# The first tokens of a transformer block: shorter Newton steps, two tiles normalised on their own, another order of the first products, and two more low parts on GpSimd

## The chip, the cores and the metric

The kernel runs on one core of one Trainium2 chip. The metric is device time in microseconds (us); the time before is 2038.93 us, the median of three runs (2038.71, 2038.93 and 2042.29).

The engines have short names below, as in the profile: PE is TensorE (matrix products and transposes), PEld its weight loads, DVE is VectorE, ACT is ScalarE, POOL is GpSimd, and SP issues most of the DMAs. Each engine works through its own queue of instructions in order and waits on semaphores for the others.

## The reference

One transformer block in float32 with 2048 tokens of 640 features, 32 heads of 20 and a feed-forward width of 1728:

```python
def _layernorm(x, axis=-1, eps=1e-5):
    m = jnp.mean(x, axis=axis, keepdims=True)
    v = jnp.var(x, axis=axis, keepdims=True)
    return (x - m) / jnp.sqrt(v + eps)

h = x + attention(_layernorm(x), wqkv) @ wo         # softmax(q k^T / sqrt(20)) v, 32 heads
h2 = h + (silu(z @ w_gate) * (z @ w_up)) @ w_down   # z = _layernorm(h)
```

## The kernel before

The tokens are cut into 16 tiles of 128 (one SBUF tile `xs[t]` of 128 x 640 each) and these into four chunks `c` of four tiles (`TPC`). Features are cut into five groups of 128 (`ND`).

Products of full float32 precision are made from two roundings: each operand `a` is kept as `a_hi`, a copy in the format fp32r, and `a_lo = a - a_hi`; a product is `a_hi w_hi + a_lo w_hi + a_hi w_lo`. The helper `split` (line 87) makes both: ACT copies to `hi`, then DVE (or POOL, by an argument) subtracts to `lo`; its instructions carry lines 88 and 89. A low part on DVE or POOL can only start behind ACT's high part.

The layer norm of a chunk takes, for each tile, `stats` (line 121): two BATCH_NORM_STATS2 over the halves of the 640 features and one BATCH_NORM_AGGREGATE into `mv`. Then `rstd_steps` (line 91) builds a list of functions that compute `r = 1/sqrt(var + eps)` for all tiles of the chunk together: `v = var + eps`, a first guess from the bits of `v`, and three Newton steps of four operations, so 14 in all; all these carry line 98. Then each tile is normalised in place (line 475), transposed on PE (`flip_tokens`, line 525; products at 529) and split into the high and low part of its columns of `z`.

**The opening** is at lines 715 to 739. SP issues the loads of four tiles of x and eight loads of `wqkv`; POOL sets the constant rows of `k_stk` (`fill_ones`, line 140, two memsets of 32 partitions x 4096). PE runs three warm-up products (line 721), which read the last tile of the chunk. `norm(0)` runs its whole list on DVE: statistics of four tiles, 14 Newton operations, four normalisations. The first two columns of weights (blocks m = 0 and 1) get their `w_hi` from ACT (line 727). Then each tile is transposed and split in turn; ahead of the last tile stands `first_blocks((0, 0))`, and after it the low parts of the weights of blocks 0 and 1 on DVE (line 734).

`first_blocks` (line 611) computes the first key block and the first query block, in two halves of 256 tokens. A pair `(h, n)` is half `h` (tokens of tiles 0 and 1, or 2 and 3) with operand pair `n`: 0 is `z_hi w_hi`, 1 is `z_lo w_hi`, 2 is `z_hi w_lo`; each pair is ten products (line 621). The remaining five pairs are issued at the first slot of the main loop (line 781). After them PE goes on with the other blocks (`query_key` and `rounds`, line 568), a stream without a pause by design.

`split_w` (called in the main loop) splits the weights of the further blocks m = 2, 3, ...: high part on ACT, low part on DVE for m < `LATE` and on POOL from `LATE` (6) on. `load_w` brings the weights in pairs of blocks into four slots, so a load on SP's queue waits until the low parts of the pair that had the slot are done. `keep` stores a finished block: a high and a low part, the latter for the widened key on POOL, and DMAs on POOL's queue to `k_d` and `q_d`.

A planner (`clock`, `takes`, `visit`) decides at build time where PE's stream takes the work of the attention's first maxima, and where a later chunk's normalisation steps go.

**Later users of the same function.** `projection` (line 886 on) uses `rstd_steps` for the second layer norm of chunks 0 to 2, during or right behind the attention, in three groups of at most five operations. `late_tokens` (line 1675 on) uses it for chunks 2 and 3 together, 8 tiles, during the first feed-forward elements: `moments` returns the list, one `apply` is added, and the loop `step` works off seven entries of this list `soon` at a time, then one entry of a list `late` at a time; these entries normalise (line 1705), transpose (line 1722) and store the late tokens.

Of the kernel before, what the change touches and what calls it, by code (L numbers as in the profile page):

```python
# [9 lines left out]
F32 = mybir.dt.float32  # L10
# [7 lines left out]
P = 128  # L18
# [5 lines left out]
ND = D // P  # L24
# [20 lines left out]
def tile_block(ctx: ExitStack, tc: tile.TileContext, x, wqkv, wo, wg, wu, wd, out):  # L45
# [41 lines left out]
    def split(src, hi, lo, lo_engine=nc.vector):  # L87
        nc.scalar.activation(hi, src, AF.Copy)  # L88
        lo_engine.tensor_tensor(out=lo, in0=src, in1=hi.bitcast(F32), op=ALU.subtract)  # L89

    def rstd_steps(pool, var, n, tag, engine=nc.vector):

        v = pool.tile([P, n], F32, name="v_" + tag)
        r = pool.tile([P, n], F32, name="r_" + tag)
        t = pool.tile([P, n], F32, name="t_" + tag)

        def some(f, *args, **kw):
            return lambda: f(*args, **kw)

        ts, tt = engine.tensor_scalar, engine.tensor_tensor  # L100
        guess = [
            some(nc.vector.tensor_scalar, v, var, EPS, None, op0=ALU.add),
            some(
                nc.vector.tensor_scalar, r.bitcast(I32), v.bitcast(I32), -0.5, 1597463007.0, op0=ALU.mult, op1=ALU.add
            ),
        ]
        better = [
            some(tt, out=t, in0=r, in1=r, op=ALU.mult),
            some(tt, out=t, in0=t, in1=v, op=ALU.mult),
            some(ts, t, t, -0.5, 1.5, op0=ALU.mult, op1=ALU.add),  # L110
            some(tt, out=r, in0=r, in1=t, op=ALU.mult),
        ]
        return r, guess + better * 3
# [4 lines left out]
            f()  # L118
        return r

    def stats(pool, src, mv):
        st = pool.tile([P, 2, 6], F32, name="st")
        for i in range(2):
            nc.vector.bn_stats(st[:, i, :], src[:, i * HALF : (i + 1) * HALF])
        nc.vector.bn_aggr(mv, st)


    NU = NG * NC
# [181 lines left out]
    with tc.tile_pool(name="pa", bufs=2) as pa:  # L310
# [99 lines left out]
        seconds, steps_due = [], [0]  # L410
        LANDING, LANDING_FIRST, SLACK, GATE, APART = 8000, 14000, 0, 500, 2500
        flips = []
        LATE, CHAIN = 6, 3000
        X_LANDING, x_there = 15000, [0]
        next_load = [0]

# [51 lines left out]
        def norm(c):  # L468

            mv = pa.tile([P, TPC, 2], F32, name="mv")  # L470
            engine, name = (nc.gpsimd, "POOL") if c else (nc.vector, "DVE")
            r, steps = rstd_steps(pa, mv[:, :, 1], TPC, "a", engine)

            def apply(t):
                nc.vector.tensor_scalar(
                    xs[c * TPC + t], xs[c * TPC + t], mv[:, t, 0:1], r[:, t : t + 1],
                    op0=ALU.subtract, op1=ALU.mult,
                )

            return (  # L480
                [
                    ("DVE", 1000, lambda t=t: stats(pa, xs[c * TPC + t], mv[:, t, :]))
                    for t in range(TPC)
                ]
                + [
                    (name if n else "DVE", 700 if n and c else 400, lambda f=f, g=g: (f(), g()))
                    for n, (f, g) in enumerate(zip(steps[::2], steps[1::2]))
                ]
                + [("DVE", 620, lambda t=t: apply(t)) for t in range(TPC)]
            )  # L490

        def flip(c, n):
# [19 lines left out]
            for b in range(2):  # L512
# [9 lines left out]
                nc.gpsimd.tensor_tensor(out=lo, in0=copy, in1=hi.bitcast(F32), op=ALU.subtract)  # L522
                takes("POOL", 4.8 * columns, clock["ACT"])

        def flip_tokens(t):

            ps = ps_wide().rearrange("p a b -> p (a b)")[:, :D]
            for k in range(ND):
                nc.tensor.transpose(
                    ps[:, k * P : (k + 1) * P], xs[t][:, k * P : (k + 1) * P], ident  # L530
                )
            ps = ps.rearrange("p (k n) -> p k n", k=ND)
            split(ps, *(z[:, :, t * P : (t + 1) * P] for z in zs[0]))

        stores = []

# [181 lines left out]
            load_w(i)  # L718
        warm = ps_one()
        for _ in range(3):  # L720
            nc.tensor.matmul(warm, ident, xs[TPC - 1][:, :CH], start=True, stop=True)
        for _, _, f in norm(0):
            f()
        zs[0] = z_tiles(0)
        first_raw = raws.pop(0), raws.pop(1)
        for m, raw in enumerate(first_raw):
            nc.scalar.activation(w_hi[:, :, m * P : (m + 1) * P], raw, AF.Copy)
        for t in range(TPC):
            flip_tokens(t)
            if t == TPC - 2:  # L730
                first_blocks((0, 0))
        for m, raw in enumerate(first_raw):
            cs = slice(m * P, (m + 1) * P)
            nc.vector.tensor_tensor(
                out=w_lo[:, :, cs], in0=raw, in1=w_hi[:, :, cs].bitcast(F32), op=ALU.subtract
            )
        load_w(4)
        loaded = 5
        split_at = (0, 4, 6, 7, 8, 9, 10, 11, 12, 13)
# [6 lines left out]
        for c in range(NC):  # L746
# [7 lines left out]
            for j, (kind, *which) in enumerate(work):  # L754
                slot[0] = 18 * c + j
                while flips and not j:
                    flips.pop(0)()
                if c == 0 and j < 9:
                    for i in range(split_at[j], split_at[j + 1]):
                        split_w(i + 2)  # L760
                        if i % 2 == 1 and loaded < 8:
                            load_w(loaded)
                            loaded += 1
                if c + 1 < NC and j == 0:
                    es[:0] = [
                        t.rearrange("p k n -> p (k n)")[:, : 2 * EW].rearrange(
                            "p (i n) -> p i n", i=2
                        )
                        for t in z_tiles(c + 1)
                    ]  # L770
                    if c:
                        es[:] = es[2:] + es[:2]
                if c + 1 < NC and j == 10:
                    es[:] = [e for e in es if any(e is own for own in own_es)]
                if j == (0 if c else 3) and c + 1 < NC:
                    load_x(c + 1)
                    x_there[0] = clock["PE"] + X_LANDING
                    lns = norm(c + 1)
                if which:
                    if (c, j) == (0, 0):  # L780
                        first_blocks((0, 1), (1, 0), (1, 1), (0, 2), (1, 2))
                        for m, ps in enumerate(firsts):
                            keep(0, m, ps)
                    else:
                        (query_key if kind == "block" else value)(c, *which)
                else:
                    flip_ctx.close()
                    psum = ps_ctx.enter_context(
                        tc.tile_pool(name="psum", bufs=1, space=bass.MemoryType.PSUM)
                    )  # L790
                    turn, jobs = [0], [0]

                    def ps_one():
                        jobs[0] += 1
                        return psum.tile([P, CH], F32, name="ps_one", tag=f"ps_{jobs[0] % 3}")

                    def ps_max():
                        n = turn[0] % 5
                        turn[0] += 1
                        if n > 2:  # L800
                            return psum_two.tile([P, CH], F32, name="ps_max", tag="ps_two")
                        return psum.tile([P, CH], F32, name="ps_max", tag="ps_max", bufs=3)

                if c == 0 and j == 6:
                    for ev in evs:
                        nc.gpsimd.memset(ev, 1.0)
                if (c, j) in ((1, 14), (1, 16), (2, 4), (3, 4)):
                    n = c if c > 1 else (j - 14) // 2
                    load_keys(0, slice(n * CH, (n + 1) * CH))
                if (c, j) in ((1, 15), (2, 0), (2, 9)):  # L810
                    load_queries(len(queries))
                if 0 in ends:
                    finish_at = min(finish_at, slot[0] + 2)
                    if slot[0] == finish_at:
                        max_finish(0)
                if j == 15 and c == 3:
                    load_values(0)
                if clock["PE"] >= x_there[0]:
# [1076 lines left out]
```

## Time and profile before

| | |
|---|---|
| median of three runs | 2038.93 us |
| profiled execution, its time | 2038.82 us |
| profiled execution, its span | 2037.0 us |
| DMA, mean over the span | 152 GB/s |
| PE, instructions | 14322 |
| POOL, instructions | 1103 |

The span runs from the first to the last instruction. A row of the timeline gives the start in us from the span's start, the length in us, the engine, the line, the operation, the tile written and the tiles read, the shape and the number of instructions merged into the row; in brackets stands the engine's idle time before it and what ended that. A row that merges several instructions gives the length of all together. A group in the list of costliest groups ends with its busy time and the mean of one instruction in ns. The list of waits says for an engine and line what it waited for: us in total, times, the longest in us.

### The profile page before, as it was taken

How to read it: one execution, taken by the hardware profiler on the slowest of the kernel's cores; microseconds unless marked ns; L12 is line 12 of the kernel's file. 1: busy time of each engine (PE TensorE's matmuls, PEld its weight loads, DVE VectorE, ACT ScalarE, POOL GpSimd, SP SyncE). 2: the span in 40 equal slices, each digit the busy share in tenths (PEclk: the TensorE clock that was granted, in tenths of full speed). 3: DMA queues.
4: the chain of work that ended last, by engine and by line, in shares of the span. 5: the costliest groups of instructions: out<-in, count | busy, mean ns of one | idle time of the engine just before them, and what ended most of it. 6: DMA issues, size and time to landing. Idle time of an engine off the chain costs nothing.

```text
span 2037.0 us, 40049 instructions
## 1 busy us (share of the span) xinstructions
PE 2012.7 (99%) x14322; PEld 1249.9 (61%) x14322; DVE 1607.9 (79%) x2826; ACT 1445.2 (71%) x2855; POOL 774.1 (38%) x1103
## 2 busy tenths in 40 slices
PE   8999999999999999999999999999999999999999
PEld 6989995343334333334333433345598888888888
DVE  5677778888888888888888888886378666676677
ACT  4677778999999999999999999987633222211221
POOL 6464423334342444352400011011146454754555
PEclk9999999999999999999999999999999999999999
DMA  7877563452634534435512131311158654974542
GB/s 244 255 244 260 175 206 89 116 161 79 187 104 124 166 115 143 149 127 176 156 46 79 27 94 44 92 62 55 33 184 302 220 192 157 344 273 158 202 150 94
DMA packets 194062, 310.01 MB, mean 152 GB/s; under 512 B 47760, under 2 KB 82576, under 8 KB 192840
## 3 DMA queue, kind: packets, MB, share of 16 engines
q1 hardware_dynamic: 187272, 283.85, 43.0%
q0 software_dynamic: 6496, 23.60, 4.0%
q8 instruction: 114, 1.87, 0.4%
q14 instruction: 84, 0.69, 0.1%
q10 hardware_dynamic: 96, 0.00, 0.0%
HBM read 207.75 MB, written 98.83 MB: 151 GB/s over the span
## 4 chain that ended last, share of the span: by engine, by line
PE 87%; DMA 3%; DVE 1%; issue 1%; POOL 1%; ACT 1%; SPq 1%; ACTq 0%; DVEq 0%; POOLq 0%
PE acc L1197 24%; PE ps_one L1187 16%; PE ps_a L1358 15%; PE ps_max L244 12%; PE ps_b L1452 8%; PE ps_one L568 6%; PE ps_max L211 2%; PE ps_max L918 2%; PE ps_b L918 1%; DMA units<-w_d 1%; DMA halves<-j_d 0%; DMA h<-in_A_x 0%; PE ps_max L953 0%; DVE tmp L1573 0%; ACT o L1207 0%
## 5 line engine op out<-in xcount | busy, mean ns | idle before, releaser
L1193 ACT ACTIVATE probs<-ps_one 128x512 f32<-128x512 f32 x2048 | 1056.7, 614 | 62.3 <-PE ps_one L1187 37.6
L250 DVE TENSOR_REDUCE mx<-ps_max 128x1 f32<-128x512 f32 x1472 | 926.2, 684 | 106.9 <-PE ps_one L1187 75.6
L1187 PE MATMUL ps_one<-q_stk,k_stk 62*128 62x512 f32 x2048 | 586.0, 450 | 2.8 <-DVE m L89 1.8
L1197 PE MATMUL acc<-probs,v_stk 128*32 128x512 f32 x4096 | 545.2, 604 | 0.0
L1187 PEld LDWEIGHTS ps_one<-q_stk,k_stk 62*128 62x128 f32 x2048 | 251.5, 184 | 432.7 <-ACT probs L1193 398.3
L244 PE MATMUL ps_max<-k_stk,q_stk 60*128 60x512 f32 x1472 | 381.2, 425 | 0.0
L244 PEld LDWEIGHTS ps_max<-k_stk,q_stk 60*128 60x128 f32 x1472 | 271.6, 186 | 24.1 <-DVE mx L250 0.9
L1573 DVE TENSOR_TENSOR tmp<-ps_a,tmp 128x512 f32<-128x512 f32 x208 | 141.2, 689 | 120.3 <-PE ps_a L1358 94.6
L233 DVE TENSOR_REDUCE mx<-ps_max 128x2 f32<-128x512 f32 x288 | 180.6, 685 | 66.5 <-PE ps_max L211 63.4
L1232 POOL TENSOR_TENSOR o<-o,rb 128x512 f32<-128x512 f32 x31 | 39.9, 1287 | 413.3 <-DMA q_stk<-q_d 241.5
L1197 PEld LDWEIGHTS acc<-probs,v_stk 128*32 128x32 f32 x4096 | 80.6, 108 | 174.8 <-issue 166.2
L223 ACT ACTIVATE ps_max<-ps_max 128x512 f32<-128x512 f32 x288 | 151.7, 583 | 47.5 <-PE ps_max L211 44.7
L1452 PE MATMUL ps_b<-halves,yp 128*128 128x320 f32 x1032 | 179.3, 308 | 2.0 <-DMA halves<-j_d 1.2
L1452 PEld LDWEIGHTS ps_b<-halves,yp 128*128 128x128 f32 x1032 | 165.1, 188 | 18.6 <-POOL yp L89 1.5
L1358 PE MATMUL ps_a<-t,units 128*128 128x512 f32 x624 | 162.6, 396 | 0.0
L1358 PE MATMUL ps_a<-z,units 128*128 128x512 f32 x516 | 133.9, 394 | 0.0
L89 POOL TENSOR_TENSOR yp<-y,yp 128x256 fp32r<-128x256 f32 x96 | 60.4, 629 | 188.2 <-ACT yp L88 188.2
L1358 PEld LDWEIGHTS ps_a<-t,units 128*128 128x128 f32 x624 | 112.6, 188 | 18.9 <-ACT tmp L1586 0.3
L1457 DVE TENSOR_TENSOR h<-ps_b,h 128x320 f32<-128x320 f32 x248 | 110.0, 481 | 6.9 <-PE ps_b L1452 5.4
L568 PE MATMUL ps_one<-z_hi,w_lo 64*128 64x512 f32 x380 | 113.7, 395 | 0.0
L568 PE MATMUL ps_one<-z_hi,w_hi 64*128 64x512 f32 x380 | 113.1, 396 | 0.0
L568 PE MATMUL ps_one<-z_lo,w_hi 64*128 64x512 f32 x380 | 111.7, 393 | 0.0
(211 smaller groups left out, 2643.3 us busy)
## 6 DMA issues: line engine op xcount, KB each, us to landing
units<-w_d SPq DMA_DIRECT2D x186, 256.0 KB
w_d<-stage SPq DMA_DIRECT2D x106, 256.0 KB
halves<-j_d SPq DMA_DIRECT2D x70, 320.0 KB
j_d<-stage SPq DMA_DIRECT2D x42, 320.0 KB
k_stk<-k_d SPq DMA_DIRECT2D x64, 160.0 KB
q_stk<-q_d SPq DMA_DIRECT2D x64, 160.0 KB
raw<-k_d SPq DMA_DIRECT2D x62, 160.0 KB
raw<-q_d SPq DMA_DIRECT2D x54, 160.0 KB
```

The costliest lines, as they stand in the source:

```text
L223: nc.scalar.activation(ps, ps, AF.Relu)
L233: nc.vector.tensor_reduce(mx[:, b, :, t, kc], ps.rearrange("p (j n) -> p j n", j=2), axis=AX.X, op=ALU.max,)
L244: nc.tensor.matmul(ps, queries[u][rows, pair, t * P : (t + 1) * P], keys[u // NC][rows, pair, kc * CH : (kc + 1) * CH], start=True, stop=True,
L250: nc.vector.tensor_reduce(mxs[u][:, b, pair, t, kc : kc + 1], ps, axis=AX.X, op=ALU.max)
L568: nc.tensor.matmul(ps, a[rows], b[rows], start=(i == n == 0), stop=(i == 1 and n == last), skip_group_check=True,)
L1187: nc.tensor.matmul(ps, keys[u // NC][rows, p, kt * P : (kt + 1) * P], queries[u][rows, p, :], start=True, stop=True,)
L1193: nc.scalar.activation(probs[p][:, b, :], ps, AF.Exp, scale=scale)
L1197: nc.tensor.matmul(acc[32 * j : 32 * j + 32, :], values[u // NC][:, kt, j * VW : j * VW + 32], probs[j // 2][:, j % 2, :], start=(kt == 0) ...
L1358: nc.tensor.matmul(ps.rearrange("p (t n) -> p t n", t=TPC), w[k][:, i], z[k][:, :, j], start=(first and m == 0), stop=(last and m == len(n ...
L1452: nc.tensor.matmul(ps, a, b, start=(n == 0), stop=(n == len(pairs) - 1))
L1457: nc.vector.tensor_tensor(out=h, in0=ps, in1=h, op=ALU.add)
L1573: add = lambda out, ps, x: nc.vector.tensor_tensor(out=out, in0=ps, in1=x, op=ALU.add)
```

## The change

Five edits, all near the opening but one:

- `rstd_steps` on DVE computes `v = -0.5 (var + eps)` at once and a first guess from its bits, and each Newton step is three operations, the last a fused `(t + 1.5) * r` of two tensors (`scalar_tensor_tensor`): 11 operations. On POOL the 14 remain.
- The first chunk's tiles 0 and 1 get statistics and Newton steps of their own on DVE; from the fourth operation on they are threaded between the statistics of tiles 2 and 3. Tiles 2 and 3 get theirs behind that: two operations on DVE, twelve on POOL.
- Tiles 0 and 1 are normalised, transposed and split first, then half 0 is multiplied with its pairs 0 and 1; then come tiles 2 and 3. The low part of the weights of block 0 stands on DVE ahead of the normalisation of tile 2, that of block 1 behind tile 3's. The remaining pairs follow as (0, 2), (1, 0), (1, 1), (1, 2).
- The warm-up products read tile 0.
- `LATE` is 4 instead of 6: the low parts of the weights of blocks 4 and 5 are POOL's.

PE's instructions stand in the same order behind the first blocks, but for the late tokens' transposes: with three operations fewer in `soon` these move one `step` forward.

```diff
         ts, tt = engine.tensor_scalar, engine.tensor_tensor
+        if engine is nc.vector:
+            first = [
+                some(ts, v, var, EPS, -0.5, op0=ALU.add, op1=ALU.mult),
+                some(
+                    ts, r.bitcast(I32), v.bitcast(I32), -0.5, 519526879.0, op0=ALU.mult, op1=ALU.add
+                ),
+            ]
+            again = [
+                some(tt, out=t, in0=r, in1=r, op=ALU.mult),
+                some(tt, out=t, in0=t, in1=v, op=ALU.mult),
+                some(engine.scalar_tensor_tensor, r, t, 1.5, r, op0=ALU.add, op1=ALU.mult),
+            ]
+            return r, first + again * 3
...
-    def stats(pool, src, mv):
+    def stats(pool, src, mv, between=()):
         st = pool.tile([P, 2, 6], F32, name="st")
+        between = list(between)
         for i in range(2):
             nc.vector.bn_stats(st[:, i, :], src[:, i * HALF : (i + 1) * HALF])
+            if between:
+                between.pop(0)()
         nc.vector.bn_aggr(mv, st)
+        for f in between:
+            f()
...
-        LATE, CHAIN = 6, 3000
+        LATE, CHAIN = 4, 3000
...
-            ps = ps.rearrange("p (k n) -> p k n", k=ND)
-            split(ps, *(z[:, :, t * P : (t + 1) * P] for z in zs[0]))
+            flipped[t] = ps.rearrange("p (k n) -> p k n", k=ND)
+
+        def flipped_hi(t):
+            nc.scalar.activation(zs[0][0][:, :, t * P : (t + 1) * P], flipped[t], AF.Copy)
+
+        def flipped_lo(t):
+            hi, lo = (z[:, :, t * P : (t + 1) * P] for z in zs[0])
+            nc.vector.tensor_tensor(
+                out=lo, in0=flipped.pop(t), in1=hi.bitcast(F32), op=ALU.subtract
+            )
...
         for _ in range(3):
-            nc.tensor.matmul(warm, ident, xs[TPC - 1][:, :CH], start=True, stop=True)
-        for _, _, f in norm(0):
+            nc.tensor.matmul(warm, ident, xs[0][:, :CH], start=True, stop=True)
+        zs[0] = z_tiles(0)
+        mv = pa.tile([P, TPC, 2], F32, name="mv")
+        r1, steps = rstd_steps(pa, mv[:, :2, 1], 2, "b")
+        r2, others = rstd_steps(pa, mv[:, 2:, 1], 2, "c", nc.gpsimd)
+        for t in range(2):
+            stats(pa, xs[t], mv[:, t, :])
+        for f in steps[:3]:
             f()
-        zs[0] = z_tiles(0)
+        stats(pa, xs[2], mv[:, 2, :], steps[3:7])
+        stats(pa, xs[3], mv[:, 3, :], steps[7:])
+        for f in others:
+            f()
...
-        for t in range(TPC):
+        for t in range(2):
+            norm_tokens(t, mv, r1, t)
             flip_tokens(t)
-            if t == TPC - 2:
-                first_blocks((0, 0))
-        for m, raw in enumerate(first_raw):
-            cs = slice(m * P, (m + 1) * P)
-            nc.vector.tensor_tensor(
-                out=w_lo[:, :, cs], in0=raw, in1=w_hi[:, :, cs].bitcast(F32), op=ALU.subtract
-            )
+            flipped_hi(t)
+        flipped_lo(0)
+        flipped_lo(1)
+        first_lo(0)
+        first_blocks((0, 0), (0, 1))
+        for t in range(2, TPC):
+            norm_tokens(t, mv[:, 2:], r2, t - 2)
+            flip_tokens(t)
+            flipped_hi(t)
+        first_lo(1)
+        flipped_lo(2)
+        flipped_lo(3)
...
-                        first_blocks((0, 1), (1, 0), (1, 1), (0, 2), (1, 2))
+                        first_blocks((0, 2), (1, 0), (1, 1), (1, 2))
```

`first_lo(m)` is the subtraction that stood in the removed loop, `norm_tokens` the one of `norm`'s former `apply`.

More of the change, by code (lines that the diff above doesn't have):

```diff
@@ L470, in norm @@
             mv = pa.tile([P, TPC, 2], F32, name="mv")
[L471 to L477, printed above, removed]
-                )
+            r, steps = rstd_steps(pa, mv[:, :, 1], TPC, "a", nc.gpsimd)
             return (
@@ L485, in norm, with norm_tokens @@
                 + [
-                    (name if n else "DVE", 700 if n and c else 400, lambda f=f, g=g: (f(), g()))
+                    ("POOL" if n else "DVE", 700 if n else 400, lambda f=f, g=g: (f(), g()))
                     for n, (f, g) in enumerate(zip(steps[::2], steps[1::2]))
                 ]
-                + [("DVE", 620, lambda t=t: apply(t)) for t in range(TPC)]
+                + [("DVE", 620, lambda t=t: norm_tokens(c * TPC + t, mv, r, t)) for t in range(TPC)]
+            )
+        def norm_tokens(tile, mv, r, t):
+            nc.vector.tensor_scalar(
+                xs[tile], xs[tile], mv[:, t, 0:1], r[:, t : t + 1],
+                op0=ALU.subtract, op1=ALU.mult,
             )
@@ L523, in flip @@
                 takes("POOL", 4.8 * columns, clock["ACT"])
+        flipped = {}
         def flip_tokens(t):
@@ L531, in flip_tokens @@
                 )
-            ps = ps.rearrange("p (k n) -> p k n", k=ND)
-            split(ps, *(z[:, :, t * P : (t + 1) * P] for z in zs[0]))
+            flipped[t] = ps.rearrange("p (k n) -> p k n", k=ND)
[5 more added lines that the diff above has]
+                out=lo, in0=flipped.pop(t), in1=hi.bitcast(F32), op=ALU.subtract
+            )
         stores = []
@@ L720, in tile_block, with first_lo @@
         for _ in range(3):
-            nc.tensor.matmul(warm, ident, xs[TPC - 1][:, :CH], start=True, stop=True)
-        for _, _, f in norm(0):
-            f()
-        zs[0] = z_tiles(0)
+            nc.tensor.matmul(warm, ident, xs[0][:, :CH], start=True, stop=True)
[6 more added lines that the diff above has]
+        for f in steps[:3]:
+            f()
+        stats(pa, xs[2], mv[:, 2, :], steps[3:7])
+        stats(pa, xs[3], mv[:, 3, :], steps[7:])
+        for f in others:
+            f()
         first_raw = raws.pop(0), raws.pop(1)
+        def first_lo(m):
+            cs = slice(m * P, (m + 1) * P)
+            nc.vector.tensor_tensor(
+                out=w_lo[:, :, cs], in0=first_raw[m], in1=w_hi[:, :, cs].bitcast(F32),
+                op=ALU.subtract,
+            )
         for m, raw in enumerate(first_raw):
             nc.scalar.activation(w_hi[:, :, m * P : (m + 1) * P], raw, AF.Copy)
-        for t in range(TPC):
+        for t in range(2):
+            norm_tokens(t, mv, r1, t)
             flip_tokens(t)
-            if t == TPC - 2:
-                first_blocks((0, 0))
-        for m, raw in enumerate(first_raw):
-            cs = slice(m * P, (m + 1) * P)
-            nc.vector.tensor_tensor(
-                out=w_lo[:, :, cs], in0=raw, in1=w_hi[:, :, cs].bitcast(F32), op=ALU.subtract
-            )
+            flipped_hi(t)
[10 more added lines that the diff above has]
+        flipped_lo(3)
         load_w(4)
```

## The prediction

> **What bounds the kernel now.** I read the page first.
>
> ```profile
> span 2037.0 us, 40049 instructions
> PE 2012.7 (99%) x14322; PEld 1249.9 (61%) x14322; DVE 1607.9 (79%) x2826; ACT 1445.2 (71%) x2855; POOL 774.1 (38%) x1103
> PE 87%; DMA 3%; DVE 1%; issue 1%; POOL 1%; ACT 1%; SPq 1%; ACTq 0%; DVEq 0%; POOLq 0%
> ```
>
> PE (TensorE) is busy 99% of the span, and the chain that ended last is PE for 87%. The change removes no PE work, so only PE's idle time can be won. The list of waits for PE has it (us in total, times, longest):
>
> ```profile
> PE ps_two L721 <- DMA xt<-in_A_x: 7.3, 1, 7.3
> PE ps_max L211 <- DVE mx L233: 4.6, 3, 2.4
> PE ps_a L1722 <- DVE z L1705: 1.0, 2, 0.8
> ```
>
> The change touches the first (the opening) and the last (the second layer norm of the late tokens). The timeline of PE in the opening (start, length):
>
> ```profile
> 7.35 4.97 PE L721 MATMUL ps_two<-xt,ident 128*128 128x512 f32 x6 [7.35 <-DMA xt<-in_A_x]
> 12.15 1.80 PE L529 MATMUL ps_wide<-ident,xt 128*128 128x128 f32 x15
> 14.25 1.45 PE L621 MATMUL ps_two<-z_hi,w_hi 128*128 128x256 f32 x10 [0.30 <-ACT z_hi L88]
> 15.54 0.71 PE L529 MATMUL ps_wide<-ident,xt 128*128 128x128 f32 x5
> 16.00 1.43 PE L621 MATMUL ps_two<-z_lo,w_hi 128*128 128x256 f32 x10
> 22.11 1.43 PE L568 MATMUL ps_one<-z_hi,w_hi 64*128 64x512 f32 x5
> ```
>
> The three warm-up products wait for tile 3 of x, then come transposes, then the first blocks from 14.25 without a gap to 22.11, where the long stream of L568 begins. Everything in the change's opening is judged by one number: how far 22.11 moves. What feeds it is on the timelines of the other engines:
>
> ```profile
> 1.38 7.05 POOL L140 MEMSET k_stk<- 32x4096 f32 x2
> 3.58 0.89 DVE L124 BATCH_NORM_STATS2 st<-xt 128x6 f32<-128x320 f32 x2 [2.70 <-DMA xt<-in_A_x]
> 4.50 0.21 DVE L125 BATCH_NORM_AGGREGATE mv<-st 128x2 f32<-128x12 f32 x1
> 4.63 0.83 DVE L124 BATCH_NORM_STATS2 st<-xt 128x6 f32<-128x320 f32 x2
> 5.49 0.21 DVE L125 BATCH_NORM_AGGREGATE mv<-st 128x2 f32<-128x12 f32 x1
> 6.38 0.89 DVE L124 BATCH_NORM_STATS2 st<-xt 128x6 f32<-128x320 f32 x2 [0.68 <-DMA xt<-in_A_x]
> 8.29 0.21 DVE L125 BATCH_NORM_AGGREGATE mv<-st 128x2 f32<-128x12 f32 x1
> 8.54 0.17 DVE L98 TENSOR_SCALAR v_a<-mv 128x4 f32<-128x4 f32 x1
> 8.74 0.17 DVE L98 TENSOR_SCALAR r_a<-v_a 128x4 int32<-128x4 int32 x1
> 11.34 2.18 DVE L475 TENSOR_SCALAR xt<-xt,mv,r_a 128x640 f32<-128x640 f32 x4
> 12.90 1.90 ACT L88 ACTIVATE z_hi<-ps_wide 128x640 fp32r<-128x640 f32 x3 [2.35 <-PE ps_wide L529]
> 17.77 1.55 DVE L734 TENSOR_TENSOR w_lo<-raw,w_hi 128x640 fp32r<-128x640 f32 x2
> 19.23 3.03 DVE L89 TENSOR_TENSOR w_lo<-raw,w_hi 128x640 fp32r<-128x640 f32 x4
> 23.68 0.74 POOL L89 TENSOR_TENSOR z_hi<-z_hi 128x256 fp32r<-128x256 f32 x1 [15.25 <-ACT z_hi L88]
> ```
>
> Statistics of four tiles, 14 Newton operations from 8.54 to 11.34 (0.20 each), then the first normalisation at 11.34; the first block starts 14.25 - 11.34 = 2.91 behind it. The eye should stop at the first row: two memsets of 3.5 us keep POOL (GpSimd) busy until 8.43. In this kernel no Newton operation meets them, since the first comes at 8.54.
>
> **The change, part by part.** *Newton for two tiles.* The chain for tiles 0 and 1 can start once tile 1's statistics are aggregated (5.49), so 0.25 later as in the rows 8.29 and 8.54: at 5.74. That is inside the second memset. Its first two operations are TENSOR_SCALAR. What such an operation does while POOL works shows elsewhere:
>
> ```profile
> 107.86 1.83 POOL L89 TENSOR_TENSOR v_stk<-v_stk 128x768 fp32r<-128x768 f32 x1 [1.86 <-ACT v_stk L88]
> 108.01 1.70 DVE L98 TENSOR_SCALAR v_a<-mv 128x4 f32<-128x4 f32 x1
> 1517.51 2.53 POOL L89 TENSOR_TENSOR y<-tmp,y 64x512 fp32r<-64x512 f32 x2 [3.25 <-ACT y L88]
> 1518.87 1.20 DVE L98 TENSOR_SCALAR r_late<-v_late 128x8 int32<-128x8 int32 x1
> ```
>
> The operation of 0.17 took 1.70: POOL ends at 109.69, it ends at 109.71. The second pair says the same (1520.04 and 1520.07). So a small TENSOR_SCALAR on DVE waits out a POOL instruction that was there first. BATCH_NORM_STATS2 does not: its rows at 3.58 and 6.38 ran beside the memset at 0.89 and 0.89 for two. Whether a memset, which reads nothing, holds a TENSOR_SCALAR as a POOL TENSOR_TENSOR does, no row shows. The bounds: no wait, or one until the memset's end, 8.43 - 5.74 = 2.7 us. I take the full wait, since the operation that waits is the same and only POOL's differs. The Trainium skill, "SBUF — State Buffer", section "Who interferes with whom", speaks against the change in the same way: `tensor_scalar` can run in a mode that takes the port pair shared with GpSimd, and then whichever started first has it for its whole instruction; only for operations with two SBUF inputs does the page except a GpSimd instruction that merely writes. By that rule v_b waits until 8.43; the two pairs of rows agree with it for reading instructions.
>
> Behind v_b on DVE stand r_b, the statistics of tiles 2 and 3, the other Newton operations and both normalisations, so all of it slides. After v_b come four BATCH_NORM_STATS2 (two take 0.83, so 1.66), two aggregations (4.50 to 4.63, 0.13 each, 0.26), and twelve small ones: ten of Newton, v_c and r_c. A dependent one costs 0.20 (8.54 to 8.74), one with another between it and its input about 0.1 to 0.13; at 0.15 they are 1.8. No row has the fused operation with two tensors; its bounds are a plain one (0.16) and two (0.40), and I take the plain one, as its work is one pass. Sum 3.7. The first normalisation then starts at 8.46 + 3.7 = 12.1 instead of 11.34 (+0.8); without the wait, at 5.74 + 0.2 + 3.7 and 0.1 for tile 2's arrival (6.38), 9.7 (-1.6). The three operations per step instead of four win 3 x 0.2 of DVE, already in the count.
>
> *Two tiles alone.* First block = first normalisation + 2.91, since z_hi of tiles 0 and 1 was and stays its last input: 15.0 (held) or 12.6 (free). From 14.25 to 22.11 PE did 60 products and 5 transposes in 7.86. Now 60 and 10 follow, so 7.86 + 0.46 (15.54 to 16.00) = 8.3: the stream begins at 23.3 (+1.2) or 20.9 (-1.2), if nothing else waits.
>
> *Tiles 2 and 3 by GpSimd.* Twelve operations behind r_c:
>
> ```profile
> 50.18 0.20 POOL L98 TENSOR_TENSOR t_a<-r_a 128x4 f32<-128x4 f32 x1
> 50.45 0.20 POOL L98 TENSOR_TENSOR t_a<-t_a,v_a 128x4 f32<-128x4 f32 x1
> 50.75 0.19 POOL L98 TENSOR_SCALAR t_a<-t_a 128x4 f32<-128x4 f32 x1
> 51.02 0.20 POOL L98 TENSOR_TENSOR r_a<-r_a,t_a 128x4 f32<-128x4 f32 x1
> ```
>
> At 0.28 apart they are 3.4, and up to 1.1 more if the two normalisations hold them. Held, they end at 12.2 + 3.4 to 4.5 = 15.6 to 16.7, while DVE is busy with two z_lo and one w_lo to about 16.7 and PE with two half blocks to 17.4; so this is hidden or costs 0.2. If POOL were 1 us slower, PE would stand 1 us before tile 2's transposes.
>
> *Order of the first blocks, warm-up on tile 0.* The products are the same, so the order costs nothing by itself: it takes the halves whose tokens exist. The warm-up now waits for tile 0 (3.58) instead of tile 3 and ends at 3.6 + 5.0 = 8.6; the first normalisation must wait for that, which it outlasts in both cases. Then PE has nothing until the first transposes, 0.8 behind the normalisation: 12.9, an idle stretch of 4.3 (held), or 10.5, 1.9 (free). What idling does to PE's clock shows in windows of 3.41 us (PE, PEld, DVE, ACT and POOL busy, then the granted clock):
>
> ```profile
> 59.48:62.89 3.41, 2.25 (x30) 1.97 (x28) 3.41 (x4) 1.88 (x5) 3.10 (x4) 1.00 0.80 244
> 124.33:127.75 3.41, 1.53 (x16) 1.21 (x14) 3.01 (x4) 0.50 (x2) 3.03 (x6) 1.00 0.93 319
> 127.75:131.16 3.41, 3.41 (x23) 3.13 (x21) 1.98 (x4) 1.78 (x5) 0.18 (x1) 0.50 0.90 250
> 4.87:8.28 3.41, 0.93 (x1) 0.50 (x2) 2.64 (x8) 0.00 (x0) 3.37 (x2) 1.00 0.98 325
> ```
>
> After a window with PE busy 1.53 of 3.41 the clock was 0.50 for the next 3.41; after one with 2.25 it stayed. That drop lost 3.41 / 2 = 1.7 us. An idle stretch of 4.3 cannot avoid a window below 1.53 wherever the windows fall, so in the held case the transposes and perhaps the first block run at half clock. The Trainium skill, "TensorE: Matmul & The Clock Gate", section "What's actually happening", says the window is free-running; so the stretch's place in it, and the loss, may differ from run to run. Bounds: nothing (the clock is back before 12.9), and 2.1 (ten transposes at 1.80 / 15 = 0.12 each and nearly as much again, 1.0; and the products of one more third of a window stretched by 1.1). I take the transposes alone, 1.0, because at half clock their own 2 us fill most of a window: held, +1.2 + 1.0 = +2.2. Free, the clock may also drop (1.9 idle and an ill-filled window): -1.2 to 0.
>
> *More low parts on GpSimd.* Two w_lo leave DVE (3.03 for four, 0.76 each) for POOL at 1.57:
>
> ```profile
> L89 POOL TENSOR_TENSOR w_lo<-raw,w_hi 128x640 fp32r<-128x640 f32 x9 | 13.9, 1572 | 0.0
> ```
>
> That is 3.1 in a stretch in which POOL idled 15.25 (row 23.68). Nothing of PE is due from them before the third block behind 22.11. Each waits for its w_hi from ACT, and behind it in POOL's queue stand the low part of the first key block (row 23.68), its stores to k_d and q_d, and the later w_lo. Held, the tokens' last z_hi ends some 2 us later than now and these two with it, near 25, when that first low part is due too, as PE is 2.2 later. Cost 0; without this cover it would be what the two run past 25, in the stores and in SP's next weight load, which waits for that slot, and in nothing of PE before the third block.
>
> *Late tokens.* The same Newton function serves the later layer norms on DVE, 11 operations instead of 14. In the last one these are entries of a list worked off seven a step, so its transposes move one step earlier on PE, with DVE, ACT, POOL and SP's stores. Same work; PE's wait there is 1.0 in all, so I bound it by -1.0 and +1.0 and take 0.
>
> **Sum.** The profiled execution took 2038.82 (1.8 around its span), 0.1 below the median of the three runs, 2038.93. 2038.8 + 2.2 = 2041.0.
>
> **The rivals.** *The memset holds nothing.* Then the opening is 0 to 1.2 shorter: 2037.6 to 2038.8, about 2038.2. For it: a memset reads nothing, and the statistics ran beside it. Against it: the same operation waited out POOL twice. This is the case that ends faster; it decides at 5.74, where v_b starts. *A second clock window is lost later.* The stretch from 59.48 was 2.25 busy and kept the clock; with the stream moved against the windows it may fall to the other side and cost 1.7 more: 2042.7, and 2043.8 with the longest cold opening. For it: of the three timed runs one is at 2042.29, 3.4 above the lowest, as two more lost windows would be; against: the other two and the profiled one lie within 0.3 of each other. *The lost window at 127.75 is spared,* by the same chance: 2041.0 - 1.7 = 2039.3. *It does not do what it says:* the free opening is eaten by the clock, 2038.8, within the first rival.
>
> **How the numbers follow.** Held, 0.57, own range 2040.0 to 2042.2 (+1.2 to +3.3); free, 0.25; second window lost, 0.11; window spared, 0.07. The range 2037.4 to 2043.4 leaves out the ends of the second and third rival. 0.2% is 4.1 us, about what a measurement of this kernel can tell from no change: slower than 2043.0 takes the long cold opening and another window, 0.10; faster than 2034.9 would take the free case with a window and the late tokens' 1.0 won, 0.03; within, 0.87.
>
> **What would show it.** v_b's length: about 2.7 ending at 8.46 (held) or 0.17. The first normalisation at 12.1, the first block at 15 to 16, L568's first product at 23.3 to 25.4; a clock of 0.50 in windows between 11 and 16. POOL's twelve done before 16.7. Late: waits of PE for z of about 1 us. Wrong it is if v_b takes 0.17, if PE stands before tile 2's transposes by over 0.5, or if the stream from 22 to 2037 is not the same length within 2 us.

## The result, and the profile after

| | before | changed |
|---|---|---|
| median, 16 runs each | 2041.27 us | 2045.88 us |
| lowest and highest | 2038.71, 2047.90 | 2041.35, 2049.07 |
| profiled execution, its time | 2038.82 | 2043.06 |
| span | 2037.0 | 2041.3 |

The ratio is 1.0019, with a 95% interval of 1.0012 to 1.0027, which is 2.4 to 5.5 us: the kernel is slower. The medians differ by 4.6 us, where 2.2 was forecast. The kernel before, run 16 times, has a median 2.3 above that of the three runs shown at first.

The list of waits for PE in the changed kernel (us in total, times, longest):

```profile
PE ps_max L229 <- DVE mx L251: 4.7, 3, 2.4
PE ps_two L747 <- DMA xt<-in_A_x: 3.9, 1, 3.9
PE ps_wide L547 <- DVE xt L503: 3.8, 1, 3.8
PE ps_a L1771 <- DVE z L1754: 2.3, 2, 1.2
```

The wait of 7.3 for x has become one of 3.9 for x and one of 3.8 for the normalised x: the warm-up products start earlier and the transposes behind them do not. The late z is waited for 2.3 instead of 1.0.

The timeline of the opening, first PE, then DVE and POOL:

```profile
3.87 4.71 PE L747 MATMUL ps_two<-xt,ident 128*128 128x512 f32 x6 [3.87 <-DMA xt<-in_A_x]
12.37 2.39 PE L547 MATMUL ps_wide<-ident,xt 128*128 128x128 f32 x10 [3.79 <-DVE xt L503]
15.56 2.50 PE L647 MATMUL ps_two<-z_hi,w_hi 128*128 128x256 f32 x10 [0.79 <-ACT z_hi L553]
17.86 2.33 PE L647 MATMUL ps_two<-z_lo,w_hi 128*128 128x256 f32 x10
22.94 1.36 PE L647 MATMUL ps_two<-z_hi,w_hi 128*128 128x256 f32 x10
26.62 1.42 PE L594 MATMUL ps_one<-z_hi,w_hi 64*128 64x512 f32 x5
...
5.92 2.54 DVE L98 TENSOR_SCALAR v_b<-mv 128x2 f32<-128x2 f32 x1
8.50 0.17 DVE L98 TENSOR_SCALAR r_b<-v_b 128x2 int32<-128x2 int32 x1
9.64 0.14 DVE L98 SCALAR_TENSOR_TENSOR r_b<-t_b,r_b 128x2 f32<-128x2 f32 x1
11.71 1.13 DVE L503 TENSOR_SCALAR xt<-xt,mv,r_b 128x640 f32<-128x640 f32 x2
16.28 0.81 DVE L764 TENSOR_TENSOR w_lo<-raw,w_hi 128x640 fp32r<-128x640 f32 x1
17.01 1.13 DVE L503 TENSOR_SCALAR xt<-xt,mv,r_c 128x640 f32<-128x640 f32 x2
...
1.38 7.05 POOL L158 MEMSET k_stk<- 32x4096 f32 x2
15.47 0.20 POOL L98 TENSOR_TENSOR r_c<-r_c,t_c 128x2 f32<-128x2 f32 x1
```

v_b, two elements per partition, takes 2.54 and ends at 8.46, 0.03 behind the memset. The first ten products take 2.50, where ten of the same form take 1.36 from 22.94 on. L594, the stream behind the first blocks (L568 before), begins at 26.62 instead of 22.11, 4.5 later; the spans differ by 4.3. So the whole difference of these two executions arises here; behind the opening each loses one window of clock, before at 127.75 and the changed kernel at 69.13. The windows of 3.41 us of the changed kernel show what slowed the products (PE, PEld, DVE, ACT and POOL busy, granted clock, then the share and GB/s of the DMAs):

```profile
7.69:11.10 3.41, 0.89 (x2) 0.06 (x1) 3.31 (x15) 1.27 (x2) 0.74 (x1) 1.00 1.09 360
11.10:14.51 3.41, 2.14 (x10) 1.99 (x10) 1.71 (x9) 0.80 (x2) 1.97 (x8) 0.50 0.91 288
14.51:17.93 3.42, 2.63 (x13) 2.37 (x12) 3.18 (x5) 0.70 (x1) 0.83 (x5) 0.50 0.01 2
17.93:21.34 3.41, 3.41 (x18) 3.41 (x18) 0.95 (x2) 0.05 (x1) 0.00 (x0) 0.50 0.28 64
21.34:24.75 3.41, 3.41 (x31) 3.41 (x30) 2.72 (x4) 3.41 (x6) 0.14 (x1) 1.00 0.36 128
```

The window in which PE idles is followed by three at 0.50, not by one. In the first two of these PE is busy 2.14 and 2.63 and the clock stays down; behind the third, which is full, it returns. The Trainium skill, "TensorE: Matmul & The Clock Gate", section "What's actually happening", has the full clock return after at least one busy window, about 3.4 us of sustained work, and gives no share of busy time for it. In these rows 2.63 of 3.41 was too little; the last section has windows of nearly that share behind which the clock did return.

### The profile page after: what moved, and what is told of

Its sections match the earlier page's. It is cut to its first block, busy times and chain, and to the rows that moved or that the text cites. A ratio compares the mean times of both kernels' runs of the same rounds, so it can differ in the third digit from the quotient of the medians.

```text
span 2041.3 us, 40049 instructions
## 1 busy us (share of the span) xinstructions
PE 2014.9 (99%) x14322; PEld 1252.7 (61%) x14322; DVE 1604.8 (79%) x2814; ACT 1445.4 (71%) x2855; POOL 781.6 (38%) x1117
## 5 line engine op out<-in xcount | busy, mean ns | idle before, releaser
L594 PE MATMUL ps_one<-z_hi,w_lo 64*128 64x512 f32 x380 | 112.2, 392 | 0.0
L594 PE MATMUL ps_one<-z_hi,w_hi 64*128 64x512 f32 x380 | 111.6, 392 | 0.1
L594 PE MATMUL ps_one<-z_lo,w_hi 64*128 64x512 f32 x380 | 110.8, 391 | 0.0
```

The costliest lines, as they stand in the source:

```text
L594: nc.tensor.matmul(ps, a[rows], b[rows], start=(i == n == 0), stop=(i == 1 and n == last), skip_group_check=True,)
```

## The experiments

The theory at the start (A): the memset held v_b, and the hole that this left on PE cost the clock. The rivals are named in each expectation. The stream's start comes from one profiled execution; ratio and mean granted clock are over the timed runs. A thousandth of the mean granted clock is 2.04 us of full clock; the part of it that falls where PE idles costs nothing.

| kernel | stream begins | ratio to before | interval | mean clock |
|---|---|---|---|---|
| before | 22.11 | 1 | | 0.9977 to 0.9983 |
| changed | 26.62 | 1.0019 | 1.0012 to 1.0027 | 0.9951 |
| e1, one memset | 21.11 | 0.9989 | 0.9980 to 0.9998 | 0.9973 |
| e2, warm-up on tile 3 | 23.56 | 0.9999 | 0.9990 to 1.0008 | 0.9975 |
| e3, e1 and five warm-ups | 21.48 | 0.9989 | 0.9979 to 0.9999 | 0.9975 |
| e4, before, warm-up on tile 0 | 24.07 | 0.9993 | 0.9984 to 1.0002 | 0.9975 |
| e5, before, one memset | 22.01 | 0.9999 | 0.9990 to 1.0008 | 0.9977 |
| e6, e1, late Newton of 14 | 21.06 | 0.9983 | 0.9974 to 0.9992 | 0.9984 |
| e7, e1, old order of pairs | 21.67 | 0.9996 | 0.9987 to 1.0005 | 0.9979 |
| e8, changed, six warm-ups | 23.02 | 0.9999 | 0.9991 to 1.0008 | 0.9978 |
| e9, changed, a filler | 24.40 | 1.0005 | 0.9996 to 1.0014 | 0.9972 |
| e10, e6 and five warm-ups | 21.47 | 0.9992 | 0.9984 to 1.0001 | 0.9974 |
| e11, e1, LATE 6 | 20.67 | 0.9989 | 0.9980 to 0.9998 | 0.9975 |

The row of before gives its mean clock in three comparisons of 27 or 33 runs. The changed kernel's 0.9951 is 0.0026 to 0.0032 below, 5.3 to 6.5 us of clock not granted: enough for its whole loss of 4.6.

**e1: the wait of v_b taken away.**

```diff
-        for b in range(2):
-            nc.gpsimd.memset(k[b * ROW + ROW // 2 : (b + 1) * ROW].bitcast(F32), 1.0)
+        nc.gpsimd.memset(k.bitcast(F32), 1.0)
```

> The changed kernel with one memset of all 128 partitions of the key stack (3.5 us) in the place of two of 32 (7.0 us), so that POOL is free at 4.9. Theory A (the memset held v_b, and the idle PE then lost its clock): v_b takes 0.17 instead of 2.54, the first normalisation starts at about 9.3 to 9.9 instead of 11.71; PE idles about 2 us instead of 3.8 before the first transposes, so the clock may still drop, but for fewer windows: the stream of L594 begins between 21.1 (clock kept) and 24 instead of 26.62, and the time is 2.5 to 5 us below the changed kernel. Rival B (the order of the first blocks and GpSimd's Newton steps cost the time, not v_b): the first normalisation is earlier but PE waits for tile 2, and the stream still begins at 25 or later.

The timeline of e1:

```profile
1.25 3.51 POOL L157 MEMSET k_stk<- 128x4096 f32 x1
6.03 0.17 DVE L98 TENSOR_SCALAR v_b<-mv 128x2 f32<-128x2 f32 x1
9.78 1.13 DVE L502 TENSOR_SCALAR xt<-xt,mv,r_b 128x640 f32<-128x640 f32 x2
10.45 1.31 PE L546 MATMUL ps_wide<-ident,xt 128*128 128x128 f32 x10 [1.38 <-DVE xt L502]
12.60 1.45 PE L646 MATMUL ps_two<-z_hi,w_hi 128*128 128x256 f32 x10 [0.84 <-ACT z_hi L552]
21.11 1.42 PE L593 MATMUL ps_one<-z_hi,w_hi 64*128 64x512 f32 x5
```

One memset of 128 partitions takes as long as one of 32, v_b takes 0.17, the normalisation starts 1.93 earlier, and the ten products take 1.45: the clock was kept, with 1.38 idle. The stream begins 5.5 earlier than in the change and 1.0 earlier than before. The ratio falls by 0.0030, some 6 us, a little more than the 2.5 to 5 expected. Rival B falls. As both the wait and the lost clock are gone here, e2 and e8 have to tell them apart.

**e2: the hole taken away, the wait left.**

```diff
-            nc.tensor.matmul(warm, ident, xs[0][:, :CH], start=True, stop=True)
+            nc.tensor.matmul(warm, ident, xs[TPC - 1][:, :CH], start=True, stop=True)
```

> The changed kernel with the warm-up products back on tile 3, which lands at about 7.4. Theory A: v_b still takes 2.5 and the first normalisation stays at 11.7, but the warm-up ends at about 12.3, right before the first transposes, so the clock is 1.00 from 11 to 15 us on; the stream of L594 begins at 23.2 to 23.8, which is 3 us earlier than in the changed kernel and 1 to 1.6 later than before. Rival B (the clock window is lost whatever the warm-up does, or the 4.5 us come from waits for DVE and POOL): the stream begins at 25.5 or later.

PE's timeline of e2:

```profile
7.72 5.43 PE L747 MATMUL ps_two<-xt,ident 128*128 128x512 f32 x6 [7.72 <-DMA xt<-in_A_x]
12.98 1.27 PE L547 MATMUL ps_wide<-ident,xt 128*128 128x128 f32 x10
15.09 1.46 PE L647 MATMUL ps_two<-z_hi,w_hi 128*128 128x256 f32 x10 [0.84 <-ACT z_hi L553]
```

Ten transposes in 1.27 instead of 2.39, ten products in 1.46 instead of 2.50. With v_b held as long (2.66, to 8.45), the stream begins at 23.56, 3.1 earlier than in the change, and the timed ratio falls from 1.0019 to 0.9999. The clock's share of the 4.5 is rather larger than 3.1: the late warm-up keeps PE until 13.15, so the transposes start 0.6 later than in the change.

**e8: the same, by a bridge.** The warm-up starts early, but goes on.

```diff
-        for _ in range(3):
-            nc.tensor.matmul(warm, ident, xs[0][:, :CH], start=True, stop=True)
+        for t in 3 * (0,) + 3 * (TPC - 1,):
+            nc.tensor.matmul(warm, ident, xs[t][:, :CH], start=True, stop=True)
```

> The changed kernel with both memsets, so v_b is held for 2.5, and with six warm-up products (three on tile 0, three on tile 3), which end at 10.5 to 12.5 and leave PE idle for less than 1.8 before the transposes at about 12.4. Theory A (the loss beyond the 1.2 of v_b is the clock): no or one window of 0.50 over the first blocks, the stream begins at 23.2 to 25, and the time is 2 to 5 us below the changed kernel, about that with the warm-up on tile 3. Rival B (the early start of the warm-up itself costs): the stream begins at 26.

PE's timeline of e8:

```profile
3.98 8.04 PE L747 MATMUL ps_two<-xt,ident 128*128 128x512 f32 x12 [3.98 <-DMA xt<-in_A_x]
12.37 1.31 PE L547 MATMUL ps_wide<-ident,xt 128*128 128x128 f32 x10 [0.35 <-DVE xt L503]
23.02 1.42 PE L594 MATMUL ps_one<-z_hi,w_hi 64*128 64x512 f32 x5
```

Transposes that start at 12.37, as in the change, now take 1.31, and the stream begins at 23.02, 3.6 earlier; the ratio is 0.9999. Here nothing else moved, so 3.6 of the 4.5 are the clock and 0.9 the rest. Starting the warm-up early does no harm; in this kernel, leaving PE without work behind it does.

**e9: why three windows and not one.**

```diff
             flipped_hi(t)
+        nc.tensor.matmul(warm, ident, xs[TPC - 1][:, :CH], start=True, stop=True)
         flipped_lo(0)
```

> The changed kernel with one more product (of the warm-up's kind, its result unused) on PE between the transposes of tiles 0 and 1 and the first block, where PE idled 0.79. It takes 0.9 at full and 1.7 at half clock. Theory A (the clock comes back only after a window in which PE hardly idles, so the hole behind the transposes and not the first stretch alone keeps it at 0.50): one window of 0.50 fewer than the changed kernel's mean of 5.8, the stream begins about 1 earlier than 26.62, at 25 to 26, though PE has more work, and the time is 0.5 to 2 us below the changed kernel's. Rival B (the number of windows is set by the idle stretch alone): as many windows, and the stream and the time 0.5 to 1.5 later than in the changed kernel.

Windows of e9:

```profile
9.00:12.42 3.42, 0.40 (x2) 0.06 (x1) 3.31 (x18) 1.36 (x2) 0.41 (x1) 1.00 1.10 361
12.42:15.83 3.41, 3.41 (x13) 2.74 (x13) 1.55 (x3) 1.41 (x2) 2.37 (x11) 0.50 0.43 138
15.83:19.24 3.41, 3.41 (x29) 3.20 (x28) 3.02 (x5) 0.07 (x1) 0.00 (x0) 1.00 0.00 0
```

The idle stretch is 3.0 and the clock drops as in the change, but the next window is full and it returns at once. The windows also fall 1.3 later here, just where the transposes begin, so these rows alone do not separate the filler from that chance; the timed runs do. With one product more to do, the stream begins 2.2 earlier than in the change (24.40), and the ratio is 1.0005, with an interval that overlaps the change's only from 1.0012 to 1.0014. The mean clock is 0.9972 instead of 0.9951, near that of the other kernels. Theory A holds with a larger effect than expected; rival B falls.

**e4: the hole alone.** The kernel before with its warm-up on tile 0.

```diff
-            nc.tensor.matmul(warm, ident, xs[TPC - 1][:, :CH], start=True, stop=True)
+            nc.tensor.matmul(warm, ident, xs[0][:, :CH], start=True, stop=True)
```

> The kernel before with one edit, the warm-up products on tile 0 as in the change: they end at 8.6 and PE idles 3.5 us until the first transposes at 12.1. Theory A (the clock): the clock is 0.50 over the transposes and first blocks, and the stream of L568 begins 2 to 4 us later than 22.11, time +2 to +4. Rival B (the idle stretch costs nothing): 22.1, time +0.

Windows of e4:

```profile
10.10:13.52 3.42, 0.65 (x6) 0.65 (x7) 2.96 (x14) 1.31 (x2) 0.00 (x0) 1.00 0.98 308
13.52:16.93 3.41, 3.41 (x18) 3.28 (x17) 2.90 (x5) 2.12 (x3) 0.00 (x0) 0.50 0.03 10
16.93:20.34 3.41, 3.41 (x31) 3.41 (x30) 1.87 (x3) 2.16 (x4) 0.00 (x0) 1.00 0.00 0
```

In the profile the hole costs one window, and the stream begins 2.0 later (24.07). That looks like the 2 to 4 expected, but 0.9 of it is not the clock's: the last tile of x landed later in this execution, so its statistics start at 8.18 instead of 7.43 and the first normalisation at 12.21 instead of 11.34:

```profile
8.18 0.89 DVE L124 BATCH_NORM_STATS2 st<-xt 128x6 f32<-128x320 f32 x2 [1.27 <-DMA xt<-in_A_x]
12.21 2.18 DVE L475 TENSOR_SCALAR xt<-xt,mv,r_a 128x640 f32<-128x640 f32 x4
```

That leaves 1.1 for the clock. The timed runs do not show even this: 0.9993, from 3.3 us faster to 0.4 slower, with a mean clock of 0.9975. That is a miss. Behind this hole PE's work had no gap and one window was lost; behind the change's it had one and three were lost. The runs of before, whose warm-up ends only as the transposes begin, may lose part of a window too, if the clock rises late in it; this is argued, and no run here separates it.

**e3 and e10: a bridge where the hole is small.** e1, and e6 below, with five warm-up products.

```diff
-        for _ in range(3):
-            nc.tensor.matmul(warm, ident, xs[0][:, :CH], start=True, stop=True)
+        for t in (0, 0, 0, TPC - 1, TPC - 1):
+            nc.tensor.matmul(warm, ident, xs[t][:, :CH], start=True, stop=True)
```

> The changed kernel with the one memset and five warm-up products (three on tile 0, two on tile 3) that bridge to the first transposes. Theory A: both losses are gone; v_b 0.17, the warm-up ends at about 10.3, the clock stays 1.00 from about 8 to 11 us on, the stream of L594 begins at 20.9 to 21.5, about 1 us earlier than before and 5 us earlier than in the changed kernel, and the time is 1 us below the kernel before. Rival B: the stream begins at 22 or later, because of GpSimd's Newton steps.

> The changed kernel with one memset, 14 Newton operations in the later layer norms and five warm-up products (three on tile 0, two on tile 3). Theory A (the bridge saves the windows that an idle stretch of 1.8 still loses in some runs): the stream begins at 20.9 to 21.5, the late z are waited for about 1.0, and the time is 2 to 4 us below the kernel before. Rival B (at 1.8 idle no window is lost, so the bridge is worth nothing): the same time as without the bridge, 3.4 us below before.

They begin the stream at 21.48 and 21.47, and neither is faster than without the bridge (0.9989 for e1 and e3; 0.9992 against 0.9983). e10 was expected 2 to 4 us below before; its ratio means 1.6 us, and its interval reaches 1. Once v_b is free, the hole is too short to need a bridge, and the bridge itself holds the transposes until 10.92, where they start at 10.45 in e1.

**e5: the memset without the change.** The edit of e1 in the kernel before.

> The kernel before with only the one memset of 128 partitions. Theory A (the memset matters only where a Newton operation meets it): no operation of DVE's opening changes, the first normalisation stays about 2.9 ahead of the first block, the stream of L568 begins at 22.0 to 22.5, the time is that of before within 1 us, so that the 2 us by which one memset with the change beats before belong to the change. Rival B (the shorter memset alone brings them): the time is 2 us below before.

Stream at 22.01, ratio 0.9999: the memset alone brings nothing, so the gain of e1 over before is the change's own.

**e7: the order of the pairs.**

```diff
-                        first_blocks((0, 2), (1, 0), (1, 1), (1, 2))
+                        first_blocks((1, 0), (1, 1), (0, 2), (1, 2))
```

> The changed kernel with one memset and the old order of the pairs behind tiles 2 and 3: (1, 0), (1, 1), (0, 2), (1, 2). Theory A (the order hides the wait for the z of tiles 2 and 3): PE waits 0.5 to 1.3 for z_hi after the second transposes, and the stream begins at 21.6 to 22.4 instead of 21.11. Rival B (the order is worth nothing): 21.1.

PE's timeline of e7:

```profile
14.59 1.28 PE L546 MATMUL ps_wide<-ident,xt 128*128 128x128 f32 x10
16.69 1.45 PE L646 MATMUL ps_two<-z_hi,w_hi 128*128 128x256 f32 x10 [0.82 <-ACT z_hi L552]
21.67 1.42 PE L593 MATMUL ps_one<-z_hi,w_hi 64*128 64x512 f32 x5
```

With the old order PE waits 0.82 for z_hi and the stream begins 0.6 later than in e1, although the transposes begin 0.5 earlier here (9.94, in e1 10.45), as x landed earlier. From the first transposes to the stream it takes 11.73 instead of 10.66, so in the profile the order is worth 1.1; the intervals of the two ratios overlap.

**e11: the low parts.** e1 with `LATE` at 6.

> The changed kernel with one memset and LATE back at 6, so the low parts of blocks 4 and 5 are on DVE. Theory A (the move costs and brings nothing): the stream begins at 21.0 to 21.3 as with one memset alone, DVE's low parts end near 21.2, the stretch from there to the first attention product is the same within 0.5 us. Rival B (two operations with two SBUF inputs on POOL slow DVE, or free it for the first key block): the stretch changes by 1 us or more.

DVE's timeline of e11:

```profile
17.62 3.02 DVE L89 TENSOR_TENSOR w_lo<-raw,w_hi 128x640 fp32r<-128x640 f32 x4
```

They end at 20.64, in front of the stream. It begins at 20.67, 0.4 ahead of e1's, because x landed earlier in this execution: from the first transposes to the stream it takes 10.66 in both (10.01 to 20.67, and 10.45 to 21.11). From the stream's start to the first product of the attention's maxima (44.92, in e1 45.33) it takes 24.25, in e1 24.22; rival B would have them differ by 1 or more. The ratio is e1's, 0.9989. So the move of the low parts shows neither a cost nor a gain.

**e6: the late tokens.**

```diff
-        if engine is nc.vector:
+        if engine is nc.vector and n == 2:
```

> The changed kernel with one memset, but with 14 Newton operations in the later layer norms, so that the late tokens' transposes stand where they stood before. Theory A (late tokens cost nothing net): PE's waits for the late z go from 2.3 back to about 1.0, and the stretch from the first feed-forward product to the end stays within 1 us of 541.9; the time is that of one memset with the change within its interval. Rival B (the earlier transposes cost about 1.3): that stretch and the time fall by 1.3.

PE's waits in e6:

```profile
PE ps_a L1770 <- DVE z L1753: 0.9, 2, 0.7
PE ps_wide L546 <- DVE xt L502: 1.8, 1, 1.8
```

The wait is back at 0.9, from 2.3 in e1. The ratio, 0.9983, is the lowest of all, 1.2 us below e1's, but the intervals overlap, and the mean clock of these runs is higher by 0.0011, which is 2.2 us and covers it. The profiles have the stretch itself. These rows begin it in e1 and e6, with the first product of the feed-forward:

```profile
1492.97 2.97 PE L1406 MATMUL ps_a<-z,units 128*128 128x512 f32 x12
1492.83 2.95 PE L1406 MATMUL ps_a<-z,units 128*128 128x512 f32 x12
```

From there to the span's end (2038.9 and 2038.1) it is 546.0 in e1 and 545.3 in e6. (The 541.9 of the expectation is counted from a product 3.5 later; from there it is 542.5 and 541.8.) Over all profiled executions it is 545.3 to 546.0 in the eight kernels with 11 operations, 545.6 in the mean, and 544.6 to 545.9 in the five with 14, 545.1 in the mean. So of the 1.4 of waiting about 0.4 shows in the time, less than rival B's 1.3; with so few executions the size is rough.

## Why the prediction was wrong

*v_b waits for the memset:* right, in place and size (2.54 for 2.7, end at 8.46). That the memset only writes did not spare this TENSOR_SCALAR. The Trainium skill's rule in "SBUF — State Buffer", section "Who interferes with whom", agrees with this and with e1, where v_b takes 0.17.

*The first normalisation:* 11.71 for 12.1; the eighteen operations behind v_b took 3.2 instead of 3.7, with the fused one at 0.14. Free: 9.78 for 9.7.

*The first block 2.91 behind it:* 2.82 in e1, but 3.85 in the change, with transposes at half clock. *The stream without a clock loss* at 23.3: 23.56 and 23.02 in e2 and e8. *Tiles 2 and 3 by GpSimd:* done at 15.67, ahead of DVE's turn for them at 17.01; hidden, as said. *The low parts:* nothing, as said (e11). *The late tokens:* taken as 0 within 1.0; the waits grew by 1.3, of which about 0.4 shows in the time (e6). *The later windows:* neither rival came, as the changed kernel's profile loses one window behind the opening, as before.

*The clock* is the step that failed. The text took 1.0 and bounded it by 2.1, "because at half clock their own 2 us fill most of a window". The transposes did fill 2.14 of 3.41, and that was not enough; behind them came 0.8 of waiting for ACT, so the next window was not full either. Measured: three windows, 3.1 to 3.6 us of the stream (e2, e8), and 0.0020 of the ratio, 4 us, in the timed runs. The mechanism was right and the term three to four times too small. The trace of before showed a return of the clock only behind a full window (127.75, 3.41 busy) and none behind a window with gaps, so there was no ground for an upper bound below several windows.

*The base* was off too. 2038.8 was taken from a profiled execution with a granted clock of 0.999, and it agreed with two of three runs; 16 runs have a median of 2041.27. The third run, 2042.29, was nearer to that than the two others. (It lies 3.6 above the lowest, not 3.4.) Of the 4.9 by which the time exceeds the forecast of 2041.0, 2.5 are the base and 2.4 the difference between the kernels, which the clock more than covers. On the right base the same sum would have given 2043.5, still 2.4 short.

*The free case,* the rival, is e1. It was right in sign and within its bounds for the stream (1.0 earlier; 0 to 1.2 forecast); the timed runs have 2.2 us.

## What to carry to other kernels

Before putting a small DVE operation earlier, look at what POOL runs at that moment: here a TENSOR_SCALAR of two elements was held 2.5 us by a memset, and all of DVE's queue waited behind it. Let the warm-up work for PE last until its real work begins, and keep what follows a hole free of gaps: here a hole and a gap of 0.8 behind it cost three windows of clock. With one memset the change has ratios of 0.9983 to 0.9996 to the kernel before in its six variants; four of the six intervals lie below 1, those of e7 and e10 reach it. What made it slower was not the idea but the wait together with the hole that it left on PE.

## What the runs showed of the hardware

How little PE work lets the clock drop, and how much brings it back, is not set by PE's busy time in the window alone. A window of e1, with PE busy 1.81 of 3.41:

```profile
8.57:11.98 3.41, 1.81 (x12) 1.08 (x10) 2.27 (x11) 2.09 (x4) 1.60 (x6) 1.00 1.10 350
```

A window of e6, with 1.65:

```profile
7.58:10.99 3.41, 1.65 (x9) 0.81 (x8) 3.05 (x15) 1.04 (x2) 0.93 (x3) 1.00 1.09 367
```

Behind both the clock was 1.00 in the next. It dropped behind 1.53 in the kernel before, but later in e1 also behind 2.48:

```profile
322.60:326.01 3.41, 2.48 (x14) 1.28 (x13) 2.28 (x4) 2.56 (x5) 3.03 (x6) 1.00 0.47 121
326.01:329.42 3.41, 3.41 (x16) 0.92 (x13) 1.90 (x3) 2.58 (x6) 3.41 (x2) 0.50 0.85 226
```

The longest idle time of PE in that window is 0.88. The return is as uneven. At half clock 2.63 did not bring the clock back in the change, and in e6 even a full window (325.02 to 328.43) was followed by another at 0.50; but in e5 a window with 2.84 did:

```profile
6.91:10.32 3.41, 2.84 (x4) 1.32 (x5) 2.80 (x13) 0.71 (x2) 0.00 (x0) 1.00 1.06 364
L720 PE MATMUL ps_two<-xt,ident x6: 592/866/1193, 7.5 to 11.1; 128*128 128x512 f32 x6
```

The 1.00 of this row is no measurement: the record of the clock begins at 10.32, and the profile prints 1.00 ahead of its first entry, as it does for 4.87 to 8.28 of the kernel before, whose record begins at 11.69. The lengths of the warm-up products (least, median and longest, in ns) tell the clock: in order they take 1.19, 1.06, 1.06, 0.67, 0.59 and 0.59, so it was half until shortly before 10.32. What else the clock goes by stays open.

The spread of the timed runs goes with the clock: the changed kernel's fastest run, 2041.35, has a mean clock of 0.997, its slowest, 2049.07, one of 0.994. The difference of 0.003 is 6.1 of their 7.7 us.

The two memsets of 32 x 4096 on POOL took 7.05 us, so 3.5 each, and one of 128 x 4096 took 3.51: four times the partitions cost no more.
